# Attention with a gated feed-forward behind it: two-bank score tiles, a later second load and later weights

## The chip, the cores and the metric

The kernel runs on one core of a Trainium2 chip. A core has five engines, each with a queue of its own that runs in order: TensorE (PE, matrix products, whose weight loads show as PEld), VectorE (DVE), ScalarE (ACT), GpSimd (POOL) and SyncE (SP, here a queue for transfers). Products land in PSUM, which has eight banks of 2 KB for each of 128 partitions; everything else is held in SBUF, and sixteen DMA engines move data, among them the transposes that this kernel makes by DMA. The metric is the device time of one execution in microseconds; the time of a kernel is the median of its runs.

## The reference

For 8 batches of 12 heads, with 448 rows of 64 elements each:

```python
q_n, k_n = rmsnorm(q, g_q), rmsnorm(k, g_k)
scores = scale * np.matmul(q_n, k_n.transpose(0, 1, 3, 2))
attn = np.exp(scores - np.max(scores, axis=-1, keepdims=True))
attn = attn / (np.sum(attn, axis=-1, keepdims=True) + 1e-09)
x = np.matmul(attn, v)                      # to (8, 448, 768)
x_prev = np.concatenate([zeros, x[:, :-1, :]], axis=1)
xk = mu_k * x + (1.0 - mu_k) * x_prev
xr = mu_r * x + (1.0 - mu_r) * x_prev
k = np.maximum(xk @ w_k, 0.0)               # 768 x 1024
r = 1.0 / (1.0 + np.exp(-(xr @ w_r)))       # 768 x 768
out = r * (k * k @ w_v)                     # 1024 x 768
```

The weights arrive as float64 words, and all products run in 16-bit floats, each operand split into a high and a low part, so that one product becomes three (high by high, high by low, low by high).

## The kernel before

The work is three streams of small steps, `attention`, `weights` and one `moe` generator for each batch. A loop at the end of the kernel always takes the next step of the stream whose clock is furthest behind; a step advances its stream's clock by a fixed rate (1/126 of a batch for attention, where `ATT_STEPS` is 126). The weights' clock starts at 0, and `moe(b)` starts when attention of batch b is done. This gives the program order. A planner then simulates the engines and puts the instructions of each engine into the order in which they would become ready, with the program order as priority; score products get a priority 400 places ahead (`QK_PRIORITY`). The order that results is fixed, and the chip runs it queue by queue.

`load(u)` issues the transfers of q and k of four heads on ScalarE's queue. `prep(u)` squares them (line 169), folds and sums the squares (lines 170 and 173), forms the inverse root by three Newton rounds of three VectorE steps each (`rsqrt`, lines 68 to 70), scales (182), splits into high and low (187, 189) and transposes by DMA (191). The sums of squares and the scratch of `rsqrt` are columns of `misc`, a PSUM tile of one bank.

Scores are made for a pair of heads in four groups. The first three hold two row tiles of 64 rows for both heads: six products of 64 rows by 128 columns, into two tiles of one bank each, one for each head. The last row tile needs one bank for both heads: six products of 64 by 64. The four banks of `sc` hold two groups at a time. For each bank VectorE takes the row maximum (line 260), ScalarE the exponential with its row sum (261), VectorE adds a small number to the sum (273) and inverts (274), ScalarE scales into the high half (279) and VectorE forms the low half (280). A DMA transpose (282, or two of 64 rows at 286) then puts the probabilities into `pT`. The scores of a group are traced ahead of the probabilities of the group before it.

`vprep(i)` prepares v of pair i: squares with their sum (206), a small product that spreads the sums over the partitions (207), their maximum (209), scales and the two halves (214, 218). `attend(i)` multiplies the transposed probabilities with v, 22 products into one bank, `av`, and ScalarE evicts them into `x` (305). The `av` bank is also used by line 207 and by the weights (416 to 422). The last two of the eight banks are `mm`, for the conversion of the weights (407 to 410) and the products of the feed-forward (line 460), which are evicted by lines 482, 516 and 519. A product's bank is free again once its last reader has run.

The lines that deal out the banks the change touches, and the two streams whose clocks it moves:

```python
misc = ps.tile([P, 512], F32, name="misc", bufs=1)
...
banks.append(ps.tile([P, 512], F32, name="sc", bufs=4))
...
av = ps.tile([P, 512], F32, name="av", bufs=1)
...
Stream([(0.0, attention)], 0.0, 1.0 / ATT_STEPS),
Stream([(0.0, lambda: wgen)], 0.0, W_RATE / (3 * NA + 1)),
```

Of the kernel before, what the change touches and what calls it, by code (L numbers as in the profile page):

```python
# [7 lines left out]
F32 = mybir.dt.float32  # L8
# [7 lines left out]
P = 128  # L16
HD = 64
NT = 7
# [15 lines left out]
ATT_STEPS = 126  # L34
# [9 lines left out]
W_RATE = 1.0  # L44
W_RATE2 = 0.41
# [27 lines left out]
def attn_moe_kernel(tc, q, k, v, g_q, g_k, mu_k, mu_r, w_k, w_v, w_r, out):  # L73
# [40 lines left out]
    nc.vector.tensor_copy(out=misc[:, 510:511], in_=gm[:, 0:1])  # L114
    rsqrt(nc, gm[:, 1:2], misc[:, 510:511], misc[:, 511:512])
# [23 lines left out]
    LD, VF, VV, TQ, SUMS, PT, SC = {}, {}, {}, {}, {}, {}, {}  # L139
# [55 lines left out]

    def vprep(i):
# [5 lines left out]
        vh = ap_.tile([P, 2, NT, HD], F16, name="vh", bufs=2)  # L202
        vl = ap_.tile([P, 2, 4, HD], F16, name="vl", bufs=2)
        vs = small.tile([P, 2], F32, name="vs", bufs=2)
        pt = ps.tile([P, 512], F32, name="av", bufs=1)
        nc.scalar.activation(out=vh[0:HD].rearrange("p h t d -> p h (t d)").bitcast(BF16), in_=vf[0:HD], func=AF.Square, accum_out=vs[0:HD, 0:1])
        nc.tensor.matmul(out=pt[:, 0:HD], lhsT=vs[0:HD, 0:1].bitcast(BF16)[:, 1:2].broadcast_to([HD, P]), rhs=ident16[0:HD, 0:HD], start=True, stop=True)
        yield
        nc.vector.tensor_reduce(out=vs[:, 1:2], in_=pt[:, 0:HD], axis=AX.X, op=ALU.max)
        sv, iv = st[:, hp:hp + 1], st[:, NP + hp:NP + hp + 1]  # L210
        nc.vector.tensor_scalar(out=sv.bitcast(I32), in0=vs[:, 1:2].bitcast(I32), scalar1=24, scalar2=23, op0=ALU.logical_shift_right, op1=ALU.logical_shift_left)
# [8 lines left out]
        if hp == NP - 1:  # L220
            batch_scales(b)
        yield
# [17 lines left out]
    def group_scores(i, t0, n):  # L240
        T = TQ[i]
        if t0 == 0:
            SUMS[i] = small.tile([P, 32], F32, name="sums")
        sums = SUMS[i]
        banks = []
        for j in range(n):
            banks.append(ps.tile([P, 512], F32, name="sc", bufs=4))
        with tc.high_priority(offset=QK_PRIORITY):
            last = None
            for m, (kl, ql) in enumerate(((0, 0), (0, 1), (1, 0))):  # L250
                for h in (1, 0):
                    hs = slice(h * HD, (h + 1) * HD)
                    last = after(last, nc.tensor.matmul,
                        out=banks[h][:, 0:S] if n == 2 else banks[0][hs, 0:S],
                        lhsT=T[hs, 1, ql * NT + t0:ql * NT + t0 + n].rearrange("p t c -> p (t c)"),
                        rhs=T[hs, 0, kl * NT:(kl + 1) * NT].rearrange("p t c -> p (t c)"),
                        start=(m == 0), stop=(m == 2))
        for j, sp in enumerate(banks):
            t = t0 + j
            nc.vector.tensor_reduce(out=sums[:, t:t + 1], in_=sp[:, 0:S], axis=AX.X, op=ALU.max, negate=True)  # L260
            nc.scalar.activation(out=sp[:, 0:S], in_=sp[:, 0:S], func=AF.Exp, bias=sums[:, t:t + 1], accum_out=sp[:, S:S + 1])  # L261
            SC[i, t] = sp
            yield

    def group_probs(i, t0, n):
        sums = SUMS[i]
        if t0 == 0:
            PT[i] = ap_.tile([P, 2, NT, S], F16, name="pT", bufs=PT_BUFS)
        pT = PT[i]
        r = sums[:, 16 + t0:16 + t0 + n]  # L270
        sps = [SC.pop((i, t0 + j)) for j in range(n)]
        for j, sp in enumerate(sps):
            nc.vector.tensor_scalar(out=r[:, j:j + 1], in0=sp[:, S:S + 1], scalar1=1e-9, scalar2=2.0 ** -15, op0=ALU.add, op1=ALU.mult)  # L273
        nc.vector.reciprocal(out=r, in_=r)
        pool, nb = (pro[0], 1) if i < NP and (4 * i + (t0 + 1) // 2) % 3 == 2 else (ap_, PH_BUFS)
        ph = pool.tile([P, 2, 2 * S], F16, name="ph", bufs=nb)
        for j in range(n):
            sp = sps[j]
            nc.scalar.activation(out=ph[:, j, 0:S], in_=sp[:, 0:S], func=AF.Copy, scale=r[:, j:j + 1])  # L279
            nc.vector.scalar_tensor_tensor(out=ph[:, j, S:], in0=sp[:, 0:S], scalar=r[:, j:j + 1], in1=ph[:, j, 0:S], op0=ALU.mult, op1=ALU.subtract)  # L280
        if n == 2:
            nc.sync.dma_start_transpose(
                out=pT.rearrange("p a c r -> p (a c) r")[:, :, t0 * HD:(t0 + n) * HD], in_=ph.rearrange("p a c -> p (a c)"))
        else:
            for h in range(2):
                nc.sync.dma_start_transpose(out=pT[:, h, :, t0 * HD:], in_=ph[h * HD:(h + 1) * HD, 0, :])
        yield

    PASSES = [(hl, c, P) for c in range(3) for hl in range(2)] + [(0, 3, P), (1, 3, P)] + [(0, c, P) for c in range(4, 7)]
# [324 lines left out]
```

## Time and profile before

| | |
|---|---|
| runs | 1214.15, 1214.28, 1221.72 us; median 1214.28 |
| the profiled execution | 1216.88 us, span 1215.1 us |
| mean granted clock of TensorE | 0.934 |
| busy: ScalarE, GpSimd | 65%, 55% of the span |
| DMA | 172.77 MB, mean 142 GB/s |
| transfers that transpose | 240 of probabilities, 96 of q and k |

The profile is one execution. Busy time is the time in which an engine ran at least one instruction, so two products that run side by side count once. A wait is idle time of an engine ahead of an instruction, put down to what released it last. TensorE overlaps a product with the next, so its busy share says little about how densely the products follow each other; the distance from one start to the next says more.

### The profile page before, as it was taken

To read this page: it belongs to the slowest core of one execution; us is meant where nothing else is said; L and a number is where in the kernel's file an instruction comes from. 1 tells how busy PE (TensorE), PEld (TensorE's weight loads), DVE (VectorE), ACT (ScalarE), POOL (GpSimd) and SP (SyncE) were. 2 spreads that over 40 slices of the span, in tenths; PEclk is the share of its full clock that TensorE was granted. 3 is DMA by queue.
4 is the path that set the end of the run, shared out by engine and by line. 5 is a ranking of instruction groups with operands and counts; after the bars stand their busy time and mean duration, and the time that the engine had idled before them with its cause. 6 is when DMAs were issued, how large, how long until landed. Compare 5 with 4: busy or idle time off the path is not lost. (4 is left out here: it accounts for less than half of the span.)

```text
span 1215.1 us, 18885 instructions
## 1 busy us (share of the span) xinstructions
PE 996.6 (82%) x5935; PEld 476.4 (39%) x5935; DVE 828.9 (68%) x2357; ACT 794.8 (65%) x1756; POOL 672.3 (55%) x678
## 2 busy tenths in 40 slices
PE   1135545686788899999999999999899799999998
PEld 0012222243344344443444444444444354445464
DVE  4577788887977577676877676857775578666200
ACT  3366668677767767677778776777687477865411
POOL 2644357645558645585657564765586257523821
PEclk9996566888989999999999999999999899999999
DMA  7898889978789878878988897797897887885001
GB/s 160 147 182 169 162 165 218 191 152 151 143 139 161 152 123 162 150 129 158 162 154 154 155 170 141 134 167 146 143 157 129 128 148 135 137 158 90 13 14 39
DMA packets 456356, 172.77 MB, mean 142 GB/s; under 512 B 411200, under 2 KB 452672, under 8 KB 456256
## 3 DMA queue, kind: packets, MB, share of 16 engines
q1 hardware_dynamic: 423328, 132.24, 64.2%
q10 hardware_dynamic: 32928, 39.34, 13.8%
q8 instruction: 46, 0.75, 0.3%
q14 instruction: 54, 0.44, 0.1%
HBM read 61.41 MB, written 11.01 MB: 60 GB/s over the span
## 5 line engine op out<-in xcount | busy, mean ns | idle before, releaser
L261 ACT ACTIVATE sc<-sc,sums 128x448 f32<-128x448 f32 x336 | 201.6, 608 | 108.0 <-DVE sums L260 99.4
L280 DVE SCALAR_TENSOR_TENSOR ph<-sc,sums,ph 128x448 f16<-128x448 f32 x336 | 218.3, 677 | 68.4 <-ACT ph L279 66.1
L238 PE MATMUL sc<-stk 64*128 64x448 f16 (+1 forms) x1152 | 190.3, 380 | 68.3 <-DVE ph L280 45.9
L460 PE MATMUL mm<-wvh,kk 128*128 128x384 f16 x896 | 236.5, 332 | 4.0 <-DVE th L519 4.0
L460 PE MATMUL mm<-xk,wkh 128*128 128x448 f16 x768 | 217.8, 363 | 11.6 <-ACT kf L482 10.1
L260 DVE TENSOR_REDUCE sums<-sc 128x1 f32<-128x448 f32 x336 | 196.3, 613 | 37.3 <-PE sc L238 36.7
L279 ACT ACTIVATE ph<-sc,sums 128x448 f16<-128x448 f32 x336 | 195.2, 642 | 31.9 <-DMA pT<-ph 10.1
L238 PE MATMUL av<-pT,vh 128*64 128x448 f16 x672 | 145.8, 387 | 63.4 <-DMA pT<-ph 49.9
L460 PE MATMUL mm<-wrh,xr 128*128 128x384 f16 x672 | 177.1, 327 | 3.1 <-ACT xr L377 2.4
L460 PEld LDWEIGHTS <-kk 128*128 128x128 f16 x1344 | 126.5, 99 | 111.2 <-issue 36.6
L460 PE MATMUL mm<-wvl,kk 128*128 128x384 f16 x448 | 148.9, 332 | 0.0
L460 PE MATMUL mm<-xk,wkl 128*128 128x448 f16 x384 | 139.2, 363 | 0.0
L189 POOL TENSOR_TENSOR nat<-qk,nat 128x896 f16<-128x896 f32 x48 | 91.3, 1903 | 67.6 <-ACT nat L187 67.6
L238 PEld LDWEIGHTS <-stk 64*128 64x128 f16 (+1 forms) x1152 | 56.0, 100 | 184.1 <-issue 138.9
L170 POOL TENSOR_TENSOR xs<-xs 128x448 f32<-128x448 f32 x48 | 55.7, 1160 | 127.1 <-ACT xs L169 126.8
L460 PEld LDWEIGHTS <-xr 128*128 128x128 f16 x1008 | 93.6, 98 | 78.8 <-issue 16.2
L375 DVE SCALAR_TENSOR_TENSOR df<-x,bsc,df 128x448 f32<-128x448 f32 x90 | 90.3, 1014 | 32.7 <-POOL df L374 32.1
L273 DVE TENSOR_SCALAR sums<-sc 128x1 f32<-128x1 f32 x336 | 49.6, 151 | 89.9 <-ACT sc L261 88.5
L182 POOL TENSOR_TENSOR qk<-qk,ss 128x896 f32<-128x896 f32 x48 | 80.1, 1689 | 54.8 <-DVE ss L70 44.7
L460 PE MATMUL mm<-wrl,xr 128*128 128x384 f16 x336 | 109.7, 327 | 0.0
L460 PEld LDWEIGHTS <-wkh 128*128 128x128 f16 x768 | 73.9, 100 | 91.3 <-issue 35.5
L238 PEld LDWEIGHTS <-vh 128*64 128x64 f16 x672 | 59.5, 117 | 113.7 <-issue 67.3
(117 smaller groups left out, 1576.8 us busy)
## 6 DMA issues: line engine op xcount, KB each, us to landing
vf<-in_v_dram SPq DMA_DIRECT2D x48, 224.0 KB, 3.8
qk<-in_k_dram ACTq DMA_DIRECT2D x48, 224.0 KB, 4.8
qk<-in_q_dram ACTq DMA_DIRECT2D x48, 224.0 KB, 5.1
out_dram<-o SPq DMA_DIRECT2D x56, 192.0 KB, 2.9
vf<-in_v_dram SPq DMA_DIRECT2D x48, 192.0 KB, 3.8
raw<-in_moe_w_k_dram ACTq DMA_DIRECT2D x16, 384.0 KB, 4.4
raw<-in_moe_w_v_dram ACTq DMA_DIRECT2D x12, 512.0 KB, 4.4
raw<-in_moe_w_r_dram ACTq DMA_DIRECT2D x12, 384.0 KB, 4.7
```

Of the source, the lines that this page charges most:

```text
L170: nc.gpsimd.tensor_tensor(out=xs[:, :, 0:HD // 2], in0=xs[:, :, 0:HD // 2], in1=xs[:, :, HD // 2:], op=ALU.add)
L182: nc.gpsimd.tensor_tensor(out=tv, in0=tv, in1=spread(y[:, 2 * NT * n:2 * NT * (n + 1)], HD), op=ALU.mult)
L189: nc.gpsimd.tensor_tensor(out=lo, in0=t4, in1=hi, op=ALU.subtract)
L238: return op(**kw)
L260: nc.vector.tensor_reduce(out=sums[:, t:t + 1], in_=sp[:, 0:S], axis=AX.X, op=ALU.max, negate=True)
L261: nc.scalar.activation(out=sp[:, 0:S], in_=sp[:, 0:S], func=AF.Exp, bias=sums[:, t:t + 1], accum_out=sp[:, S:S + 1])
L273: nc.vector.tensor_scalar(out=r[:, j:j + 1], in0=sp[:, S:S + 1], scalar1=1e-9, scalar2=2.0 ** -15, op0=ALU.add, op1=ALU.mult)
L279: nc.scalar.activation(out=ph[:, j, 0:S], in_=sp[:, 0:S], func=AF.Copy, scale=r[:, j:j + 1])
L280: nc.vector.scalar_tensor_tensor(out=ph[:, j, S:], in0=sp[:, 0:S], scalar=r[:, j:j + 1], in1=ph[:, j, 0:S], op0=ALU.mult, op1=ALU.subtract)
L375: nc.vector.scalar_tensor_tensor(out=df, in0=xc, scalar=sc[:, MX + j:MX + j + 1], in1=df, op0=ALU.mult, op1=ALU.add)
L460: nc.tensor.matmul(out=ps_, lhsT=la(i, a), rhs=ra(i, c), start=(i == 0 and a + c == 0), stop=(i == n - 1 and a == 1))
```

## The change

The PSUM is dealt out anew. `misc` and `av` go: the sums of squares move to a tile in SBUF (`sst`), and everything that used `av` takes a bank of `mm`, of which there are still two. The six banks that are left form three score tiles of two banks each.

A group is now always a whole two-bank tile. Four heads have seven groups: three of the first pair, one that holds the last row tile of both pairs (twelve products of 64 by 64, the second pair's with its halves swapped over the partitions), three of the second pair. VectorE takes both maxima of a group in one instruction, adds the small number to both sums in one, and inverts both in one. Exponentials, scalings, low halves and transposes are as many as before.

The squares of v move to the end of the pair before (`vsquare`), the small product behind the last product of `attend` into free columns of the same bank (`vsum`), and ScalarE copies its result to SBUF before VectorE takes the maximum there. `load(1)`, which fetches q and k of heads 4 to 7, is traced after `prep(0)` and not before it. The weights' clock starts at 0.03, and attention counts 123 steps to a batch. The mixing for the feed-forward (`early_mix`) is divided over two groups of three parts and not three of two.

```diff
-ATT_STEPS = 126
+ATT_STEPS = 123
+W_START = 0.03
...
-    misc = ps.tile([P, 512], F32, name="misc", bufs=1)
...
-        pt = ps.tile([P, 512], F32, name="av", bufs=1)
+        pt = ps.tile([P, 512], F32, name="mm", bufs=MM_BUFS)
...
     def prep(u):
         y = small.tile([P, NSS], F32, name="ss", bufs=2)
-        o = (u % 2) * 2 * NSS
-        ss, tm = misc[:, o:o + NSS], misc[:, o + NSS:o + 2 * NSS]
+        sst = small.tile([P, 2 * NSS], F32, name="sst", bufs=2)
+        ss, tm = sst[:, 0:NSS], sst[:, NSS:]
...
+    def vsquare(i):
+        vf = VF[i]
+        vh = ap_.tile([P, 2, NT, HD], F16, name="vh", bufs=2)
+        vs = small.tile([P, 2 + HD], F32, name="vs", bufs=2)
+        nc.scalar.activation(out=vh[0:HD].rearrange("p h t d -> p h (t d)").bitcast(BF16), in_=vf[0:HD], func=AF.Square, accum_out=vs[0:HD, 0:1])
+        VS[i] = vh, vs
+
+    def vsum(i, dst):
+        vs = VS[i][1]
+        nc.tensor.matmul(out=dst, lhsT=vs[0:HD, 0:1].bitcast(BF16)[:, 1:2].broadcast_to([HD, P]), rhs=ident16[0:HD, 0:HD], start=True, stop=True)
+        nc.scalar.copy(out=vs[:, 2:], in_=dst)
...
+    def scores(g):
+        u, x, t0 = g
+        both = ps.tile([P, 2, 512], F32, name="sc", bufs=3)
+        sums = small.tile([P, 4], F32, name="sums", bufs=6)
         with tc.high_priority(offset=QK_PRIORITY):
             last = None
             for m, (kl, ql) in enumerate(((0, 0), (0, 1), (1, 0))):
-                for h in (1, 0):
...
+                for i in (2 * u + x,) if t0 < NT - 1 else (2 * u, 2 * u + 1):
+                    T = TQ[i]
+                    for h in range(2):
+                        hs = slice(h * HD, (h + 1) * HD)
+                        if t0 < NT - 1:
+                            dst, n = both[:, h, 0:S], 2
+                        else:
+                            o = (h + i % 2) % 2 * HD
+                            dst, n = both[o:o + HD, i % 2, 0:S], 1
+                        last = after(last, nc.tensor.matmul, out=dst,
...
+        nc.vector.tensor_reduce(out=sums[:, 0:2], in_=both[:, :, 0:S], axis=AX.X, op=ALU.max, negate=True)
+        SC[g] = both, sums
+        for j in range(2):
+            nc.scalar.activation(out=both[:, j, 0:S], in_=both[:, j, 0:S], func=AF.Exp, bias=sums[:, j:j + 1], accum_out=both[:, j, S:S + 1])
+            yield
...
+        nc.vector.tensor_scalar(out=r, in0=both[:, :, S], scalar1=1e-9, scalar2=2.0 ** -15, op0=ALU.add, op1=ALU.mult)
         nc.vector.reciprocal(out=r, in_=r)
...
     def attend(i):
...
-        av = ps.tile([P, 512], F32, name="av", bufs=1)
+        av = ps.tile([P, 512], F32, name="mm", bufs=MM_BUFS)
...
+        if i + 1 < len(pairs):
+            with tc.issue_after(last.ins):
+                vsum(i + 1, av[:, S:])
...
         load(0)
         vload(0)
+        yield
+        yield from prep(0)
         load(1)
-        yield
-        yield from prep(0)
+        vsquare(0)
...
-        Stream([(0.0, lambda: wgen)], 0.0, W_RATE / (3 * NA + 1)),
+        Stream([(0.0, lambda: wgen)], W_START, W_RATE / (3 * NA + 1)),
```

More of the change, by code (lines that the diff above doesn't have):

```diff
@@ L221, in vprep @@
             batch_scales(b)
+        if i + 1 < len(pairs):
+            vload(i + 1)
         yield
@@ L250, in group_scores @@
             for m, (kl, ql) in enumerate(((0, 0), (0, 1), (1, 0))):
-                for h in (1, 0):
[L252 to L262, printed above, removed]
-            yield
[L265 to L273, printed above, removed]
+                for i in (2 * u + x,) if t0 < NT - 1 else (2 * u, 2 * u + 1):
[8 more added lines that the diff above has]
+                        last = after(last, nc.tensor.matmul, out=dst,
+                            lhsT=T[hs, 1, ql * NT + t0:ql * NT + t0 + n].rearrange("p t c -> p (t c)"),
+                            rhs=T[hs, 0, kl * NT:(kl + 1) * NT].rearrange("p t c -> p (t c)"),
+                            start=(m == 0), stop=(m == 2))
@@ L274, in group_probs @@
         nc.vector.reciprocal(out=r, in_=r)
-        pool, nb = (pro[0], 1) if i < NP and (4 * i + (t0 + 1) // 2) % 3 == 2 else (ap_, PH_BUFS)
+        pool, nb = (pro[0], 1) if u < NP // 2 and gi % 3 == 2 else (ap_, PH_BUFS)
         ph = pool.tile([P, 2, 2 * S], F16, name="ph", bufs=nb)
[L277 to L280, printed above, removed]
@@ L343, in attention @@
             if gi + 1 < len(groups):
-                yield from group_scores(*groups[gi + 1])
-            yield from group_probs(i, t0, n)
-            if t0 == 6:
+                yield from scores(groups[gi + 1])
+            yield from probs(g, gi)
+            if done:
                 yield from attend(i)
             b, hp = pairs[i]
-            if hp == NP - 1 and t0 >= 2:
+            if hp == NP - 1 and t0 in (2, 4):
                 yield from early_mix(b, t0)
-            if t0 == 6 and hp == NP - 1:
-                DONE.append(b)
+                if done:
+                    DONE.append(b)
     def early_mix(b, t0):
```

97 lines of the change are left out of this document (49 added, 48 removed).

## The prediction

> **What bounds the kernel now.** The page comes first (span, slices, chain), then busy time by stage, then TensorE's waits in each stage, then single stretches in order of time.
>
> ```profile
> span 1215.1 us, 18885 instructions
> PE 996.6 (82%) x5935; PEld 476.4 (39%) x5935; DVE 828.9 (68%) x2357; ACT 794.8 (65%) x1756; POOL 672.3 (55%) x678
> PE   1135545686788899999999999999899799999998
> 60.00:240.00 180.00, 90.23 (x458) 40.76 (x456) 144.56 (x444) 120.78 (x253) 94.74 (x84) 0.71 0.90 180
> 420.00:1080.00 660.00, 618.49 (x3775) 289.91 (x3774) 475.81 (x1320) 476.15 (x1081) 391.94 (x403) 0.98 0.85 147
> 1147.66 54.76 PE mm L460 x330
> ```
>
> The columns of a stage are its length, then busy time (and count) of PE, weight loads, DVE, ACT and POOL, granted clock, DMA share, GB/s. There are three stages. Until about 240 us TensorE is half idle, its clock is 0.71, and VectorE is the fullest engine (144.56 of 180, 80%). From 420 on TensorE is busy for 618.49 of 660 us (94%) and no other engine passes 73%; the DMA share is 0.85, but the change moves the same bytes in as many transfers. At the end 330 products of the last batch run alone, at 54.76/330 = 0.166 us each, as densely as they ever do. So a microsecond of TensorE's queue saved after about 420 is a microsecond of the total; one saved earlier counts in part, by bringing the full stage forward.
>
> In that stage TensorE loses time to waits and to short bursts:
>
> ```profile
> PE av L238 <- DMA pT<-ph: 21.4, 19, 2.1
> PE sc L238 <- DVE ph L280: 12.9, 8, 6.8
> PE mm L460 <- ACT kf L482: 1.8, 2, 1.3
> PE mm L460 <- DVE th L519: 1.7, 3, 0.9
> ...
> PE sc L238 <- DVE ph L280: 14.1, 12, 4.3
> ...
> PE av L416 <- ACT x L305: 2.9, 1, 2.9
> ```
>
> The first four rows are TensorE's waits in 420 to 1080 us (us, times, longest), the last two those in 200 to 420. Scores wait for the probabilities of an earlier group to free their PSUM: 12.9 + 14.1 = 27 us. The expert products, in two banks of `mm`, wait 1.8 + 1.7 us for evictions.
>
> ```profile
> 66.34 0.53 PE L238 MATMUL sc<-stk 64*128 64x448 f16 x1 [6.02 <-DVE ph L280]
> ...
> 615.48 0.36 PE L238 MATMUL sc<-stk 64*128 64x448 f16 x1
> 615.77 0.38 PE L238 MATMUL av<-pT,vl 128*64 128x448 f16 x2
> 615.98 0.36 PE L238 MATMUL av<-pT,vh 128*64 128x448 f16 x2
> 616.27 0.74 PE L238 MATMUL sc<-stk 64*128 64x448 f16 x5
> 616.94 0.38 PE L238 MATMUL av<-pT,vh 128*64 128x448 f16 x1
> 617.25 1.05 PE L238 MATMUL sc<-stk 64*64 64x448 f16 x7
> 618.22 0.57 PE L238 MATMUL av<-pT,vh 128*64 128x448 f16 x3
> ...
> 1109.87 0.36 PE L238 MATMUL sc<-stk 64*128 64x448 f16 x1
> ```
>
> TensorE in order of time: a group of six score products is cut into one and five, with other work between. The lone one takes 615.77 - 615.48 = 0.29 us, the five 616.94 - 616.27 = 0.67, together 0.96. The six of a group in one bank run whole: the seven of the row at 617.25 (those six and a lone one) take 618.22 - 617.25 = 0.97, less 0.29 is 0.68. A cut costs 0.28 us. Counted over the trace, 96 of the 144 two-bank groups are cut (the first and the last stand above), and none of the 48 one-bank groups.
>
> **The change part by part.** Times are against the profiled execution: 1216.9 us, span 1215.1; the median of the runs is 1214.28, 2.6 below.
>
> (1) *One tile of two banks per group.* Both banks now come free together, as the one bank of a last group did, so I take the cuts as gone: 96 x 0.28 = 27 us, and (1110 - 420)/(1110 - 66), two thirds, of it after 420: **-18** (bounds 0, if the cuts stay, and -27).
>
> (2) *Shared last group.* Per four heads, two bursts of six products become one of twelve: 24 in all. Two at a time, nothing but a change of mode is saved: next to 0. Four at a time a second 0.68 us goes: 24 x 0.68 = 16. Midway 8, two thirds after 420: **-5**. The Trainium skill (TensorEngine Tiling (Array Packing), Key Properties) says that a change of tiling mode drains the engine, and lists four independent tiles of 64x64; by that page the sum would have 16 here. It also says (Gotcha 1) that different row tiles cannot use one PSUM bank at once. The row at 617.25 shows two row tiles writing one bank within the time of one product, so the trace speaks against that sentence as long as the partitions differ.
>
> (3) *Third tile.* The 27 us of score waits can go whole or stay whole: scores are put ahead of other work, so the planner will again issue them as soon as a bank is free in its plan, and VectorE can again be later than planned. Half: **-13** (0 to -27). Next late after that are the products with the transposed probabilities (21.4 us), which the change leaves as they are.
>
> (4) *VectorE.*
>
> ```profile
> L260 DVE TENSOR_REDUCE sums<-sc 128x1 f32<-128x448 f32 x336 | 196.3, 613 | 37.3 <-PE sc L238 36.7
> L209 DVE TENSOR_REDUCE vs<-av 128x1 f32<-128x64 f32 x48 | 10.3, 215 | 6.8 <-PE av L207 6.8
> L273 DVE TENSOR_SCALAR sums<-sc 128x1 f32<-128x1 f32 x336 | 49.6, 151 | 89.9 <-ACT sc L261 88.5
> L218 DVE SCALAR_TENSOR_TENSOR vl<-vf,bstat,vh x96: 459/482/1912, 22.7 to 1100.9; 128x256 f16<-128x256 f32 x96
> L375 DVE SCALAR_TENSOR_TENSOR df<-x,bsc,df x90: 657/816/2461, 217.9 to 1149.6; 128x448 f32<-128x448 f32 x90
> L280 DVE SCALAR_TENSOR_TENSOR ph<-sc,sums,ph x336: 658/675/686, 65.6 to 1117.5; 128x448 f16<-128x448 f32 x168
> L68 DVE TENSOR_TENSOR misc<-misc,ss x72: 169/194/196, 25.6 to 1007.5; 128x28 f32<-128x28 f32 x72
> L218 DVE SCALAR_TENSOR_TENSOR vl<-vf,bstat,vh 128x256 f16<-128x256 f32 x96 | 62.1, 686 | 15.2 <-ACT vh L214 15.1
> ```
>
> Rows with a bar give busy us and mean ns; rows with slashes the shortest, median and longest ns. 336 maxima become 168 over twice the elements: by the two reduce rows an element costs (613 - 215)/384 = 1.04 ns, so one of 896 takes 613 + 448 x 1.04 = 1077, and 206 us become 181: 25 saved. 336 small scalings become 168: 168 x 0.151 = 25. 192 reciprocals become 168: 24 x 0.151 = 4, taken at the price of a small scaling. Sum 54 saved. Against it, the sums of squares move from PSUM to SBUF. Lines 218 and 375 read two SBUF tensors, and reach 1912 and 2461 ns at a least time of 459 and 657; line 280, with one of its two in PSUM, never passes 686, and line 68, now of that second kind, never 196. After the change the 9 root steps of each of the 24 preparations (216) are of the first kind. By line 218 (mean 686, median 482) each gains 0.20 us: 44; the 4 scalings beside them (96) may gain half as much: 10. VectorE is left where it was, 829 - 54 + 54: **0**. The bounds hold for the stage of 60 to 240 us, where VectorE is the fullest and a sixth of its work stands: -9 without any contention, +20 if the steps meet GpSimd more often than line 218 does, since GpSimd waits for their result in turn. The rule is in the Trainium skill (SBUF — State Buffer, Who interferes with whom): a VectorE instruction with two SBUF inputs contends with GpSimd's reads, one with a single SBUF input outside the two-port modes does not. Rows and page agree.
>
> (5) *ScalarE.* 48 small copies of 64 elements are added; the trace has none, so between a fraction and the whole of line 209's 0.215 (as many elements, on the other engine): 0 to 10 us on an engine that is busy 72% in the full stage: 0, with 10 as the bound. The squares and sums of v keep their number; `vload` of the next pair is issued after the last reader of the single `vf`, as the wait for that reader demanded before, in the same SP queue.
>
> (6) *The `av` bank goes; its users share the two `mm` banks.*
>
> ```profile
> 603.11 0.33 PE L460 MATMUL mm<-wrh,xr 128*128 128x384 f16 x1
> ...
> 607.73 0.87 ACT L516 ACTIVATE th<-mm,bsc 128x128 f32<-128x128 f32 x3
> 608.72 0.34 PE L460 MATMUL mm<-wrh,xr 128*128 128x384 f16 x1
> ```
>
> A product finished at 603.44 is evicted by 608.60, and the next user of that bank starts at 608.72: evictions can lag 5 us, because ScalarE works in order. So far the other bank covered it. With 48 attention products in the same two banks, one of them waits, or makes the next product wait. Queued behind it on TensorE is everything. From below: 0, as the present two banks cost 1.8 + 1.7 us in 660. From above: the one wait in the trace on an eviction from the shared `av` bank, 2.9 us, for each of 48: 139. I take 0.3 us each, **+15**, nearest the lower end, since the planner places work by when banks come free.
>
> (7) *Start.*
>
> ```profile
> 11.28 0.95 ACT L169 ACTIVATE xs<-qk 128x896 f32<-128x896 f32 x1 [8.44 <-DMA qk<-in_k_dram]
> 12.99 1.26 ACTq L150 DMA_DIRECT2D qk<-in_k_dram  x2
> 18.74 0.51 ACT L407 ACTIVATE mm<-raw 128x384 f32<-128x384 f32 x1 [4.76 <-DMA raw<-in_moe_w_k_dram]
> 19.18 0.93 ACT L169 ACTIVATE xs<-qk 128x896 f32<-128x896 f32 x1
> 57.90 2.42 PE L238 MATMUL sc<-stk 64*128 64x448 f16 x12 [17.98 <-DMA stk<-nat]
> ...
> L170 POOL TENSOR_TENSOR xs<-xs 128x448 f32<-128x448 f32 x48 | 55.7, 1160 | 127.1 <-ACT xs L169 126.8
> L182 POOL TENSOR_TENSOR qk<-qk,ss 128x896 f32<-128x896 f32 x48 | 80.1, 1689 | 54.8 <-DVE ss L70 44.7
> L189 POOL TENSOR_TENSOR nat<-qk,nat 128x896 f16<-128x896 f32 x48 | 91.3, 1903 | 67.6 <-ACT nat L187 67.6
> ```
>
> The first scores run at 57.90, 46.6 us after the preparation began. On the way, q's squares (19.18) stand behind a weight conversion that waited 4.76 us for its load. In series the preparation has two squares (0.95, 0.93), two folds (1.16 each), two scalings (1.69 each), two remainders (1.90 each) and some 13 short VectorE steps of 0.19 (line 68): 14 us. With the reductions and the transposes I estimate 20: at best -26. At worst nothing changes: the row at 12.99 is the load of heads 8 to 11, issued far ahead of its place in the program, so the planner can pull the moved load forward too. Weights come later by 0.03 of a first batch, at most 0.03 x 240 = 7 us on the first expert product. VectorE still has the same work to do before 240 us. **-8** (+7 to -26).
>
> Sum: -18 - 5 - 13 + 0 + 0 + 15 - 8 = -29: 1216.9 - 29 = 1188, and 1185 against the median.
>
> **The rivals.**
> - *Banks bind (slower).* If each of the 48 attention products costs 1.5 us of TensorE in (6), that is 72 and not 15: 1185 + 57 = 1242. It turns slower than before at 15 + 29 = 44 us, 0.9 us each. For it: the 5 us lag. Against it: the small waits on `kf` and `th`.
> - *Nothing left over.* The SBUF reads of (4) cost the upper bound (+20), and VectorE, later by that, keeps the score waits (0 for -13) and the start (0 for -8) as they were: 1185 + 20 + 13 + 8 = 1226; with half of these 1205. Centre 1214. For it speaks the tail of lines 218 and 375; against it, that each step lasts only 0.19 us. The loads not moving belongs here too. The page's port rule (SBUF — State Buffer in the Trainium skill) is this rival's mechanism.
> - *All of it.* Full bounds of (3) and (7), four at a time in (2), no contention and no bank waits: -18 - 11 - 27 - 26 - 9 = -91, so 1123 against the median, and up to 1150 with a part of it missing.
>
> **How the numbers follow.** About 1% (12 us) is what a measurement here can tell from no change. Forecast 0.52, with its own range of 1165 to 1202; all of it 0.13; nothing left over 0.17; banks bind 0.18. So faster 0.65, same 0.17, slower 0.18. The likeliest time is 1185. From 1140 to 1235 half of the best case (0.06) and half or more of the worst (0.11) are left out.
>
> **What would show it.** Right: score products in runs of six and twelve, no runs of one and five; fewer score waits on `ph`; 168 maxima near 1077 ns; first scores before 50 us. (4): the root steps with medians near 0.2 and a tail over 0.5 us. (6): waits of `mm` on `x`, `th` and `kf` in 420 to 1080, under 20 us in all. The prediction is wrong if these pass 45, if runs of one and five stay, or if the stage before 240 us grows.

## The result, and the profile after

The changed kernel takes 1314.59 us (median; 1314.36 to 1314.75), the kernel before 1214.22 us beside it: 1.083 times as long, with a 95% interval of 1.076 to 1.090. The forecast was 1185, with a range to 1235. The profiled execution took 1314.68 us, its span 1312.8, which is 97.7 more than before.

From the page of the changed kernel (span, TensorE by slices, the chain that ended last), and from its busy time by stage, with the columns of before:

```profile
span 1312.8 us, 18533 instructions
PE 955.5 (73%) x5935; PEld 479.6 (37%) x5935; DVE 852.0 (65%) x1996; ACT 810.7 (62%) x1804; POOL 671.8 (51%) x678
PE   1233453458596778888887778978788789999998
...
DMA 26%; DVE 19%; PE 15%; ACT 13%; issue 7%; POOL 5%; SPq 2%; ACTq 0%; POOLq 0%; DVEq 0%
...
60.00:240.00 180.00, 72.26 (x428) 32.19 (x427) 145.47 (x393) 122.33 (x263) 93.24 (x80) 0.70 0.88 176
420.00:1080.00 660.00, 529.25 (x3350) 259.13 (x3350) 467.27 (x1069) 467.71 (x1064) 376.38 (x383) 0.94 0.81 144
```

As many matmuls as before (5935), but from 420 to 1080 us only 3350 of them run, in 529 us, where there were 3775 in 618. In the slices TensorE has two single nines, and a row of them only from about 1083 us on, near the end. The chain that ended last goes through transfers (26%) and VectorE (19%) more than through TensorE (15%): most of the span is set by the latencies of attention. From 420 to 1080 us no engine is full: TensorE, the busiest, is at 529 of 660 us (80%).

A table by progress shows where the 98 us are. A batch's attention is done when its last pair is evicted into `x`. The lengths come from the starts of those evictions in the trace (the 6th, 12th, 24th and 48th), in us:

| kernel | batch 1 | batch 2 | 3 and 4 | 5 to 8 | behind the last | span |
|---|---|---|---|---|---|---|
| before | 212 | 151 | 255 | 509 | 87 | 1215 |
| changed | 223 | 180 | 262 | 507 | 141 | 1313 |

So the loss is 11 us in the first batch, 29 in the second, 4 in all of the six others, and 54 behind the last attention. Two views give the ends of that last stretch. The first two rows are the evictions into `x` (shortest, median and longest ns, first and last start), before and changed. The last two are the expert products alone, that is the products of the feed-forward, in the stretch behind them, before and changed (length, then busy us and count of PE and of weight loads, clock, DMA share, GB/s).

```profile
L305 ACT ACTIVATE x<-av,bstat x48: 614/637/732, 91.0 to 1128.0; 128x448 f32<-128x448 f32 x48
```

```profile
L316 ACT ACTIVATE x<-mm,bstat x48: 636/652/702, 89.2 to 1172.1; 128x448 f32<-128x448 f32 x48
```

```profile
1128.00:1215.00 87.00, 80.48 (x470) 45.78 (x468) 0.98 0.08 19
```

```profile
1172.00:1313.00 141.00, 133.33 (x786) 76.81 (x786) 0.99 0.08 20
```

When attention is done, 786 expert products are left and not 470. 316 products by 0.166 us are 52 us. The feed-forward has fallen behind attention, by 316 of the 438 that a batch has.

The waits of the changed kernel, over the whole span (us, times, longest), first TensorE's and then ScalarE's:

```profile
PE sc L245 <- DVE ph L286: 121.3, 49, 14.5
PE mm L431 <- DVE wf L425: 68.1, 16, 8.6
PE mm L475 <- ACT x L316: 23.3, 13, 3.8
PE mm L475 <- ACT kf L497: 16.1, 11, 2.8
...
ACT ph L285 <- DMA pT<-ph: 71.1, 44, 4.8
ACT vh L198 <- DMA vf<-in_v_dram: 30.0, 29, 2.0
```

Scores wait 121 us for their tiles, though there is a third. TensorE's queue runs in order, and a wait shows only as far as the planner's order has nothing else ahead of the product that waits; so this row also says that expert products were missing as a cover. The row of `wf` has grown from 15.4 to 68.1 us: the statistics of the weights, which now take a bank from the pool of the expert products, wait for their own operand, the converted weights. ScalarE waits 71 us for `ph` to be free of its transposes, where it was 10. The rows of before for scores, the statistics, `ph` and v, over the whole span:

```profile
PE sc L238 <- DVE ph L280: 45.9, 27, 6.8
...
PE av L416 <- DVE wf L410: 15.4, 4, 8.1
...
ACT ph L279 <- DMA pT<-ph: 10.1, 9, 2.0
...
ACT vh L206 <- DMA vf<-in_v_dram: 4.6, 3, 2.2
```

### The profile page after: what moved, and what is told of

It reads as the page before. It is cut to its first block, busy times and chain, and to the rows that moved or that the text cites. A ratio compares the mean times of both kernels' runs of the same rounds, so it can differ in the third digit from the quotient of the medians.

```text
span 1312.8 us, 18533 instructions
## 1 busy us (share of the span) xinstructions
PE 955.5 (73%) x5935; PEld 479.6 (37%) x5935; DVE 852.0 (65%) x1996; ACT 810.7 (62%) x1804; POOL 671.8 (51%) x678
## 4 chain that ended last, share of the span: by engine, by line
DMA 26%; DVE 19%; PE 15%; ACT 13%; issue 7%; POOL 5%; SPq 2%; ACTq 0%; POOLq 0%; DVEq 0%
PE mm L475 13%; DMA pT<-ph 11%; DMA stk<-nat 7%; DVE ph L286 4%; DMA qk<-in_q_dram 4%; DVE sums L267 4%; ACT ph L285 3%; ACT sc L270 3%; DMA vf<-in_v_dram 2%; DVE df L390 2%; DVE vl L223 2%; ACT nat L185 1%; PE mm L245 1%; ACT vh L219 1%; POOL nat L187 1%
## 5 line engine op out<-in xcount | busy, mean ns | idle before, releaser
L286 DVE SCALAR_TENSOR_TENSOR ph<-sc,sums,ph 128x448 f16<-128x448 f32 x336 | 225.7, 678 | 158.4 <-ACT ph L285 154.7
L285 ACT ACTIVATE ph<-sc,sums 128x448 f16<-128x448 f32 x336 | 210.1, 637 | 108.6 <-DMA pT<-ph 71.1
L245 PE MATMUL sc<-stk 64*128 64x448 f16 (+1 forms) x1152 | 141.3, 395 | 145.1 <-DVE ph L286 121.3
L475 PE MATMUL mm<-wrh,xr 128*128 128x384 f16 x672 | 181.5, 338 | 11.4 <-ACT x L316 6.0
L267 DVE TENSOR_REDUCE sums<-sc 128x2 f32<-128x896 f32 x168 | 181.0, 1080 | 8.4 <-PE sc L245 8.2
L245 PE MATMUL mm<-pT,vh 128*64 128x448 f16 x672 | 125.8, 397 | 24.4 <-DVE wf L425 8.9
L475 PEld LDWEIGHTS <-xr 128*128 128x128 f16 x1008 | 99.4, 101 | 89.9 <-issue 28.5
L245 PEld LDWEIGHTS <-stk 64*128 64x128 f16 (+1 forms) x1152 | 46.4, 103 | 216.6 <-issue 166.7
L499 POOL TENSOR_TENSOR kf<-kf 128x448 f32<-128x448 f32 x64 | 60.7, 949 | 93.6 <-ACT kk L498 93.6
L535 POOL TENSOR_TENSOR o<-th,bsc 128x384 f32<-128x384 f32 x48 | 41.4, 862 | 113.5 <-DVE th L534 75.6
```

What stands on the lines that cost most here:

```text
L245: return op(**kw)
L267: nc.vector.tensor_reduce(out=sums[:, 0:2], in_=both[:, :, 0:S], axis=AX.X, op=ALU.max, negate=True)
L285: nc.scalar.activation(out=ph[:, j, 0:S], in_=both[:, j, 0:S], func=AF.Copy, scale=r[:, j:j + 1])
L286: nc.vector.scalar_tensor_tensor(out=ph[:, j, S:], in0=both[:, j, 0:S], scalar=r[:, j:j + 1], in1=ph[:, j, 0:S], op0=ALU.mult, op1=ALU.sub ...
L475: nc.tensor.matmul(out=ps_, lhsT=la(i, a), rhs=ra(i, c), start=(i == 0 and a + c == 0), stop=(i == n - 1 and a == 1))
L499: nc.gpsimd.tensor_tensor(out=kf, in0=kf, in1=kf, op=ALU.mult)
```

## The experiments

They are named e1 to e18. A time without an interval is that of one execution; the kernel before took 1211 to 1214 us beside each. Times with an interval are medians, and the interval is that of the ratio to the kernel before.

**The parts alone, in the kernel before.** Sharing: all users of `av` take a bank of `mm`.

```diff
-ps.tile([P, 512], F32, name="av", bufs=1)
+ps.tile([P, 512], F32, name="mm", bufs=MM_BUFS)
```

> The kernel before with one edit: everything that used the av bank takes one of the two mm banks; misc and the four one-bank score tiles stay. If sharing the two banks is what costs (theory S), this alone gives most of the 100 us: 1270 to 1320, with waits of expert products on the eviction of x, and weight products waiting ahead of scores. If the cost is the root steps in SBUF (theory P) or the new groups and the third tile (theory T), it stays within 1200 to 1235.

e1: 1310.05 us, +99. A loss as large as that of the whole change comes from this one edit, made at four places. It shares a little more than the change does: here the 48 sums of v take tiles of the pool too, where the changed kernel puts them into the tile of `attend`. The same edit for only a part of the users:

> The kernel before with one edit: only the Gram products of the weights go from the av bank to the two mm banks; v's sums and attend keep av. The weights end at about 293 us, so theory S-early (the loss starts where the weights' tiles, held by a late VectorE, keep attention waiting) gives 1240 to 1270 here and all of it before 400 us. Theory S-late (what costs is attend among the expert products) gives 1205 to 1225.

> The other half: attend and the sums of v go to the two mm banks, the weights keep the av bank for themselves. S-late: 1270 to 1310, lost evenly over the batches, because a product of 22 matmuls and its eviction hold one of two banks 48 times. S-early: 1215 to 1245. If the two halves together fall clearly short of the 99 us of sharing everything, the loss needs both.

Only the statistics of the weights (e5): 1231.59, +20, between the two ranges. Only attention and the sums of v (e6): 1287.76, +76, in the upper range, but not spread evenly over the batches: of 71 us more span, 50 lie behind the last attention. Together the two make 96 of the 99.

The sums of squares in SBUF:

```diff
-        ss, tm = misc[:, o:o + NSS], misc[:, o + NSS:o + 2 * NSS]
+        sst = small.tile([P, 2 * NSS], F32, name="sst", bufs=2)
+        ss, tm = sst[:, 0:NSS], sst[:, NSS:]
```

> The kernel before with one edit: sums of squares and root scratch in an SBUF tile, the misc bank left empty. Theory P (VectorE loses to GpSimd at the shared ports, and what waits for it loses too): the root steps grow from 60 us to about 117 as in the changed kernel, and the time to 1240 to 1280. Theory S or T: the steps grow likewise but the time stays within 1205 to 1230, as VectorE has room after 240 us.

e2: 1243.50, +32. The start (the load of heads 4 to 7 behind `prep(0)`, the weights' clock at 0.03):

```diff
+W_START = 0.03
...
         yield from prep(0)
+        load(1)
```

> The kernel before with two edits: load(1) traced after prep(0), the weights' clock from 0.03. My prediction: 8 us less, first scores before 50 us, 1200 to 1210. If the planner pulls the load forward anyway: 1214 within 8. If the later weights hold back the first expert products: 1220 to 1235.

> The kernel before with the moved load and later weights once more, in rounds. If the 12 us of the single look are real: a ratio of 0.985 to 0.995 with an interval below 1. If they were the luck of one run: an interval that holds 1.

e3: 1199.28, -12, and over four executions (e12) 1201.42 (ratio 0.989, 0.983 to 0.994): the one part that gains, and the fastest kernel here.

**The other parts, on that start.** The shared last group, with one-bank tiles and v as before:

> The kernel before with the moved load and later weights (1199) and, on top, the shared last group with its seven groups for four heads; one-bank score tiles, and v as before. Theory G (the shared group is what costs in the 1277 of the changed structure on the old banks): 1250 to 1280. Theory V (the moved squares and sums of v cost): 1195 to 1215.

e9: 1255.05, in theory G's range. The squares and sums of v at the end of the pair before:

> The other half: the kernel before with the moved load and later weights and, on top, v as in the changed kernel (load right after the last reader, squares at the end of the pair before, the sum behind attend, the copy on ScalarE); groups as before. Theory V: 1240 to 1280, with ScalarE's wait of the squares for v's load near the 56 us seen with the changed structure. Theory G: 1195 to 1215.

e10: 1228.94, between the two ranges. These two are not clean: the edits change how many steps a batch of attention has, and so how far its clock runs (114 of 123 and 126 of 126, where before has 120 of 126 and the changed kernel 117 of 123), and with that the program order against the feed-forward. The two together have the clock of the changed kernel: the changed code on the banks of before (four one-bank score tiles, `av`, `misc`).

> The changed kernel with the banks of before: four score tiles of one bank, av and misc back, so what stays of the change is the shared last group, the moved squares and sums of v, the moved load and the later weights. If these are harmless, 1195 to 1215, as the moved load and later weights alone gave 1199 against 1211. If the shared group (probabilities of two pairs at once, four transposes in a row) costs: 1230 to 1290.

e8: 1276.66, so the shared group and the moved v cost 77 over the 1199.28 of the start alone. ScalarE's wait for v stands out there:

```profile
ACT vh L200 <- DMA vf<-in_v_dram: 56.3, 32, 6.5
```

**The score tiles, in the changed kernel.** Two wide tiles and an `av` bank of its own; and six tiles of one bank with a maximum each in the place of three wide ones.

```diff
-        both = ps.tile([P, 2, 512], F32, name="sc", bufs=3)
+        both = ps.tile([P, 2, 512], F32, name="sc", bufs=2)
...
-        av = ps.tile([P, 512], F32, name="mm", bufs=MM_BUFS)
+        av = ps.tile([P, 512], F32, name="av", bufs=1)
```

> The changed kernel with two score tiles of two banks and the av bank back for everything that used it (seven banks in use). Theory S: the 100 us go, 1200 to 1240. Theory P or T, which both stay in this kernel: 1270 or more; a loss of the third tile alone would show as still longer score waits on the low halves.

> The changed kernel with its three two-bank score tiles taken apart into six tiles of one bank, each with its own maximum and its own small scaling (so VectorE gets back about 48 us of work). Theory T (a two-bank tile is held until its last reader, which lets the next scores start late and makes the row maximum wait for both heads): 1250 to 1290. If the width of the tile is harmless or good: 1315 to 1345, for the added VectorE work.

e4: 1369.19, 55 slower than the changed kernel, although `av` has a bank of its own again; theory S's 1200 to 1240 are far off. The third tile is worth at least that, if a bank of its own for `av` costs nothing. Its next limit is in ScalarE's wait for `ph`, which is 2.5 us with two wide tiles, 71.1 with three, and 98.1 with six tiles of one bank (first two, then six):

```profile
ACT ph L285 <- DMA pT<-ph: 2.5, 2, 1.9
```

```profile
ACT ph L288 <- DMA pT<-ph: 98.1, 69, 6.3
```

The six one-bank tiles (e7) take 1340.77, so the wide tile with one maximum is worth 26.

**Why does sharing cost so much?** Is it the number of banks? Three banks for `av` and `mm` together, as many as before, but in one pool, on the start of e3:

```diff
-MM_BUFS = 2
+MM_BUFS = 3
...
-ps.tile([P, 512], F32, name="av", bufs=1)
+ps.tile([P, 512], F32, name="mm", bufs=MM_BUFS)
```

> The kernel before with the moved load and later weights, and the av bank and the two mm banks made one pool of three. If the loss by sharing is a matter of the number of banks, pooling three costs nothing: 1190 to 1210. If it is the mixing of long-held attention products with the expert products whatever the number, 1225 to 1290.

e11: 1295.91 (ratio 1.066, 1.061 to 1.071), 94 over e12, which has the same start and the same three banks under two names, and above the range for mixing. The number of banks is not it. TensorE's waits in e11, and in e3 behind them:

```profile
PE mm L239 <- DMA pT<-ph: 71.9, 23, 10.5
PE sc L239 <- DVE ph L281: 65.4, 48, 5.7
```

```profile
PE av L239 <- DMA pT<-ph: 48.1, 32, 4.7
PE sc L239 <- DVE ph L281: 33.2, 24, 7.0
```

Counted from the trace of e11, in 13% of the time from 430 to 1070 us no expert product holds a bank, though attention holds one of the three at most; in e3 that share is 0.3%.

The order of TensorE's instructions in the compiled kernels shows a difference. Tiles are numbered as the program makes them. Before, 143 of the 293 tiles of `av` and `mm` start ahead of a tile made earlier; on the average 6.1 expert tiles start ahead of an attention product that the program places before them. In every kernel with one pool it is none: 0 of 246 in the changed one, 0 of 293 in e1 and e11. In these kernels a pool is dealt out in program order. Theory A: expert products wait behind attention products, or sums of v, that are ahead of them in the program and cannot run yet. The next two kernels trace the product of a pair one score group later, with the pool and, as a control, without.

```diff
-            if t0 == 6:
+            if later is not None:
+                yield from attend(later)
+                later = None
+            if t0 == 6 and hp == NP - 1:
                 yield from attend(i)
+            elif t0 == 6:
+                later = i
```

> The start edits and the pooled three banks of e11 (1295.9 us), and one thing more: the attention product of a pair is traced one score group later, behind the first probabilities of the next pair (not at the end of a batch). Banks of one name are handed out in the order of the program: in the issued order of e11 no tile of the pool starts ahead of an earlier one, where with separate banks 146 of 293 do. Theory A (an attention product placed in the program before its transposed probabilities are there holds back the expert products behind it): with the product later in the program the pool costs much less, 1215 to 1250. Theory B (the cost is something else: too few banks, or slow evictions): 1285 to 1305, as e11.

> Control: the same later attention product with the separate banks of before and the start edits (e3 and e12, 1199 to 1201 us). Both theories: no gain, 1195 to 1210, since a separate bank does not hold back the expert products. If it gains as much as e13 does, theory A is wrong.

e13: 1298.51 (1.066 to 1.078) with the pool, no better than e11; e14: 1226.40 (1.007 to 1.015) without, slower by 25 than e12. Theory A's numbers for e13 are missed, and those of the control too. Against its own control the pool costs 72 us here (1298.51 less 1226.40), where it costs 94 with the product in its old place. The 22 us less are theory A's direction, but only a quarter of the price. One group of 24 in a batch is about one expert tile of 22, and six to seven would have to pass, so the dose was small; that was not foreseen. In the changed kernel:

> The changed kernel (1314.6 us) with the attention product one group later in the program, and the sum of squares of v in a bank of its own turn of the pool (it was in that product's bank). Theory A: a good part of the some 97 us for mixing comes back, 1230 to 1280. Theory B: 1300 to 1330.

> The changed kernel with the same two banks, but named apart: one for attention, the sums of v and the weights' statistics, one for the expert products and the weights' conversion. Theory A: what mixing costs comes back, some 95 us, less what one bank for the expert products costs: each of the 160 or so expert groups then waits for its eviction, at the 0.9 us of an eviction 140 us at most and a part of it hidden: 1270 to 1350. Theory B (too few banks): clearly slower than the changed kernel, 1380 or more.

e15: 1373.47 (1.127 to 1.137) with the product later and the sums of v in tiles of their own, so worse by 59, and beyond both ranges. With the two banks named apart (e16) 1446.59, which is theory B's number and not A's. But one bank for the expert products is a new bound (193 us are left behind the last attention), so this kernel doesn't tell the theories apart. The last two move the program order by the feed-forward's clocks alone. In the kernel `moe(b)` starts a quarter of a batch (`LAG`; 0.2 for the first, `LAG0`) behind the point of its clock at which attention of batch b is due; here it starts there at once and lasts 0.8 of a batch. With separate banks, the planner's order leaves 0.8 expert tiles ahead of each attention product by these clocks, and not 6.8; that kernel was not run.

```diff
-LAG = 0.25
-LAG0 = 0.2
-MOE_DUR = 1.0
+LAG = 0.0
+LAG0 = 0.0
+MOE_DUR = 0.8
```

> The pooled three banks of e11 (1295.9 us) with another program order and nothing else: the feed-forward of a batch starts on its stream's clock as soon as its attention is done (0.25 of a batch sooner) and lasts 0.8 of a batch there. Moving the attention product alone by one group (e13) was too little by the issued order: with separate banks, some 6.8 expert tiles later in the program start ahead of each attention tile (e3), and with these clocks 0.8 do. Theory A (tiles of one name are handed out in program order, so expert products that could run wait for attention products ahead of them in the program): most of the 97 us of e11 over e3 comes back, 1200 to 1240. Theory B (mixing costs by something else: evictions, conflicts of the two in one pool): 1280 to 1305.

> The changed kernel (1314.6 us) with the same clocks for the feed-forward, and nothing else. Theory A: most of the some 97 us for sharing comes back, 1215 to 1260; with it the kernel would be about where the kernel before is. Theory B: 1300 to 1330.

e17: 1280.02 (1.053 to 1.058); e18: 1353.40 (1.114 to 1.123). Both miss theory A's numbers; e17 stands at the edge of B's range, e18 beyond it. The table by progress says what the order did:

| kernel | batch 1 | batch 2 | 3 and 4 | 5 to 8 | behind the last | span |
|---|---|---|---|---|---|---|
| e3, start, two names | 200 | 148 | 254 | 505 | 91 | 1198 |
| e1, shared | 226 | 175 | 256 | 514 | 137 | 1308 |
| e11, one pool of three | 211 | 156 | 268 | 526 | 133 | 1294 |
| e17, e11 with the clocks | 217 | 180 | 267 | 523 | 93 | 1279 |
| changed | 223 | 180 | 262 | 507 | 141 | 1313 |
| e18, changed with the clocks | 228 | 196 | 300 | 532 | 95 | 1351 |
| e2, sums in SBUF | 221 | 147 | 270 | 516 | 87 | 1242 |
| e8, changed, banks of before | 207 | 167 | 249 | 526 | 126 | 1275 |
| e9, start and shared group | 196 | 170 | 242 | 516 | 130 | 1253 |
| e4, two wide tiles, own `av` | 238 | 161 | 304 | 577 | 87 | 1367 |

The stretch behind the last attention, in expert products (first e11, then e17):

```profile
1162.00:1294.00 132.00, 126.60 (x753) 73.38 (x750) 0.99 0.09 22
```

```profile
1187.00:1279.00 92.00, 86.57 (x510) 49.61 (x507) 0.99 0.09 22
```

Program order alone took the backlog from 753 to 510 products, about e3's 496, and the end stretch from 133 to 93. But attention ended 25 us later, nearly all of it in the second batch. In the changed kernel the end stretch shrinks by 46 too, and attention is 84 later. So the order of the program decides which of the two streams is late. A backlog is not the pool's alone, either: e8 and e9, with `av` apart, leave 715 and 697 expert products behind the last attention. Counted as above, 1.3 and 3.4 expert tiles start ahead of an attention product there, and 6.8 in e3.

What is shown: mixing costs 94 to 99 us at either number of banks (e1, a single execution, and e11); a pool lets no tile pass another; a change of the program order alone moves the loss from the end into attention. What stays open: no order tried here gives back more than 16 us of that (22 against its own control), so that the in-order pool is the whole of it is argued and not shown. What the clocks of e17 cost with separate banks is not known. An order by clocks that differ between the first batches and the later ones, and more buffers for `ph`, were not tried either. And in the changed kernel itself the price of sharing was not measured: each kernel tried there that names the banks apart has fewer of them elsewhere, or the four narrow score tiles of before.

## Why the prediction was wrong, step by step

It had the sign wrong. The step that failed most is (6): it put +15 for the shared banks, where e1 measures 99. The rival with the right sign, banks that bind, said 1242 with 1.5 us for each attention product. For attention and the sums of v alone (e6) 76/48 = 1.6 us were measured, so its price was near, though not for the reason that it gave, the lag of evictions (see (6)). The statistics of the weights in the same banks, 20 us by e5, stood in no term.

- **What bounds the kernel.** The reading that a microsecond saved on TensorE's queue is one saved in all held for the kernel before. That it would stay the bound after the change was the assumption under every later term. TensorE's queue was full because expert products filled the waits of attention. With the change they no longer do: attention loses 40 us in the first two batches and keeps its pace from there on, while the feed-forward falls 316 products behind.
- **(1), no more cuts: right.** By the order in the trace all runs of score products are of six or a multiple of it; none of one or five is left. What that saves in time was not measured by itself. The matching row, and one of the shared groups with the start behind it:

```profile
616.59 0.74 PE L245 MATMUL sc<-stk 64*128 64x448 f16 x6
617.26 0.36 PE L475 MATMUL mm<-xk,wkh 128*128 128x448 f16 x1
...
598.03 0.76 PE L245 MATMUL sc<-stk 64*64 64x448 f16 x12
598.72 0.55 PE L475 MATMUL mm<-xk,wkh 128*128 128x448 f16 x2
```

- **(2), the shared group.** Twelve products take 0.69 us, as six do (617.26 - 616.59 = 0.67): four at a time, so TensorE saves the upper value, 24 x 0.68 = 16 us. The step left out what else a shared group does: it holds rows of two pairs and alters the order of attention. With the moved v it costs 77 (e8); its own part was not measured cleanly.
- **(3), the third tile: the step that asked what is late next named the wrong one.** Score waits rose from 45.9 us (whole span) to 121.3. Not the products with `pT` came next, but the two buffers of `ph`: 10.1 to 71.1 us.
- **(4), VectorE: one sum right by luck, the time wrong.** VectorE's busy time was to stay at 829 us and is 852. The maxima are at the forecast length, 1080 ns for 1077. But the 206 us that the step starts from are 336 times 613 ns, and their busy time was 196.3, since neighbours overlapped: 15 us are saved and not 25. The steps on the squares in SBUF grew by 57 us, from 60 to 117 (the seven groups of before, then the changed ones), forecast 54. That is luck: the 216 root steps grew by 26, forecast 44, and the 96 scalings by 31, forecast 10.

```profile
L68 DVE TENSOR_TENSOR misc<-misc,ss 128x28 f32<-128x28 f32 x72 | 13.6, 189 | 1.0
L69 DVE SCALAR_TENSOR_TENSOR misc<-misc,ss 128x28 f32<-128x28 f32 x72 | 13.5, 188 | 0.7
L70 DVE SCALAR_TENSOR_TENSOR ss<-misc,ss 128x28 f32<-128x28 f32 x72 | 13.0, 181 | 0.7
...
L176 DVE TENSOR_SCALAR misc<-misc,gm 128x14 f32<-128x14 f32 x24 | 7.0, 293 | 0.3
...
L65 DVE TENSOR_SCALAR misc<-misc 128x28 int32<-128x28 int32 x24 | 4.5, 188 | 0.2
L66 DVE TENSOR_SCALAR ss<-misc 128x28 int32<-128x28 int32 x24 | 4.4, 181 | 0.3
L175 DVE TENSOR_SCALAR misc<-misc 128x14 f32<-128x14 f32 x24 | 4.1, 172 | 0.1
```

```profile
L267 DVE TENSOR_REDUCE sums<-sc 128x2 f32<-128x896 f32 x168 | 181.0, 1080 | 8.4 <-PE sc L245 8.2
...
L69 DVE TENSOR_TENSOR sst<-sst,ss 128x28 f32<-128x28 f32 x72 | 24.9, 346 | 0.7
L70 DVE SCALAR_TENSOR_TENSOR sst<-sst,ss 128x28 f32<-128x28 f32 x72 | 21.8, 303 | 0.7
L173 DVE TENSOR_SCALAR sst<-sst 128x14 f32<-128x14 f32 x24 | 21.2, 883 | 0.4
L71 DVE SCALAR_TENSOR_TENSOR ss<-sst,ss 128x28 f32<-128x28 f32 x72 | 19.0, 264 | 0.6
L66 DVE TENSOR_SCALAR sst<-sst 128x28 int32<-128x28 int32 x24 | 11.1, 463 | 0.1
L174 DVE TENSOR_SCALAR sst<-sst,gm 128x14 f32<-128x14 f32 x24 | 10.2, 425 | 0.2
L67 DVE TENSOR_SCALAR ss<-sst 128x28 int32<-128x28 int32 x24 | 8.5, 355 | 0.3
```

  The larger error was to set the loss off against the saving in busy time: the root steps are links of a chain that the next scores wait for. Alone they cost 32 us (e2), above the bound of 20; the wide tile with one maximum gives 26 (e7). These rows agree with the port rule of the Trainium skill (SBUF — State Buffer, Who interferes with whom): the root steps with two SBUF inputs reach 2004 ns, where line 68 on `misc` never passed 196. The rule was used rightly; what it costs in time was mis-drawn.
- **(5), ScalarE and v.** The copies are just above the upper bound of 10 us:

```profile
L204 ACT COPY vs<-mm 128x64 f32<-128x64 f32 x48 | 10.7, 223 | 12.6 <-PE mm L203 9.7 <-PE mm L475 1.1 <-PE mm L436 1.0
```

  The failing sentence is that `vload` keeps its order and so costs nothing. In its new place the square sits at the head of ScalarE's in-order queue while its load is under way: 29 waits, 30.0 us, where 4.6 were. Everything of attention on ScalarE is queued behind it. In e10, which moves v and nothing else of the change's code, the same wait is 33.0 us, and 4.4 in e3.
- **(6), shared banks: right place, wrong mechanism, wrong size.** +15 was forecast (0 to 139) and 94 to 99 measured. The forecast priced the wait of an attention product for an eviction. These waits exist: of `mm` products on `x`, `kf` and `th` there are 45.5 us from 420 to 1080, past the limit of 45 that the prediction set itself:

```profile
PE mm L475 <- ACT x L316: 17.5, 8, 3.8
PE mm L475 <- ACT kf L497: 15.8, 10, 2.8
...
PE mm L475 <- DVE th L534: 7.0, 5, 4.6
PE mm L475 <- ACT th L531: 5.2, 4, 2.4
```

  But three banks cost as much as two (e11), and there these waits are 2.5 us in the same stretch, less than the 11.0 of e3:

```profile
PE mm L239 <- DVE th L520: 1.4, 1, 1.4
...
PE mm L461 <- ACT kf L483: 1.1, 1, 1.1
```

  So evictions are not the main price of a pool. "The planner places work by when banks come free" was the step that failed: with one name no tile starts ahead of one made earlier (0 of 246 here), where 143 of 293 did before. That this lost freedom is the whole price stays open.
- **(7), the start: right alone.** -8 was forecast and -12 measured (-21 to -7 by the interval of e12), though the first scores come at 51.84 us in e3 and not before 50. In the changed kernel the gain is gone before the first batch ends, at 223 us and not 212; a longer stage before 240 us was a sign of being wrong that the prediction had named. Its first scores run at 51.15 us and not 57.90:

```profile
51.15 3.54 PE L245 MATMUL sc<-stk 64*128 64x448 f16 x18
```

The parts do not add: 99 + 32 + 77 - 12 = 196, and the change costs 100. That e1 alone comes so near to the whole is therefore in part chance. The third wide tile pays part of the rest back; how much is overlap wasn't separated.

## What to carry to other kernels

Before two kinds of work are put into one pool of buffers, count in the issued order how often a later tile of the one starts ahead of an earlier tile of the other: that freedom was lost here with two buffers and with three. On a full engine ask what fills its waits, since the bound moves when the filler is tied to the work it covers. And a microsecond saved beside the path doesn't pay for one added on a chain, even on the same engine.

## What was not expected of the hardware

A scaling of 14 elements with one input had a median of 170 ns in PSUM, and 934 in SBUF (158 at least, 1833 at most), longer than the two-input steps beside it (188). The same row, before and changed, and the two-input step of line 69:

```profile
L175 DVE TENSOR_SCALAR misc<-misc x24: 163/170/181, 24.5 to 1003.8; 128x14 f32<-128x14 f32 x24
```

```profile
L69 DVE TENSOR_TENSOR sst<-sst,ss x72: 167/188/2004, 23.7 to 1056.8; 128x28 f32<-128x28 f32 x72
...
L173 DVE TENSOR_SCALAR sst<-sst x24: 158/934/1833, 14.2 to 1030.3; 128x14 f32<-128x14 f32 x24
```

In the trace, 13 of the 24 meet GpSimd's scaling by the gains (line 170, 2.08 us) and 7 another GpSimd instruction; all these 20 end 29 to 36 ns behind the end of a GpSimd instruction, as if they had waited for it. The other four take 158 to 166 ns. The Trainium skill (SBUF — State Buffer, Who interferes with whom) lists this operation among those that can take both ports, and the trace agrees with that; no run here takes GpSimd away to test it. The prediction had counted half of a two-input step's rise for it.

Twelve score products of 64 by 64 into two banks took the time of six of 64 by 128, with two of them writing one bank on different partitions. And the granted clock followed TensorE's busy share in this stage: 0.98 at 618 of 660 us before, 0.94 at 529 in the changed kernel, so the stage that lost the cover also ran its products on a slower clock.
